# Sigmoid attention and a gated feed-forward in one kernel: four changes of order and buffer around a TensorE that is already full

## The chip, the cores and the metric

The kernel runs on one core of one Trainium2 chip. The metric is the device time of a run in microseconds (us). A run's span, from its first to its last instruction, is about 1.8 us shorter. Every run also lists its mean granted TensorE clock (1.0 is full speed).

## The reference

```python
# q, k, v: (8 batches, 12 heads, 448 positions, 64)
scores = scale * np.matmul(q, k.transpose(0, 1, 3, 2)) - np.log(448)
attn = 1.0 / (1.0 + np.exp(-scores))
attn_out = np.matmul(attn, v)
x = attn_out.transpose(0, 2, 1, 3).reshape(3584, 768)
gate = np.maximum(x @ w_gate, 0.0)          # 768 -> 1536
out = (gate * (x @ w_val)) @ w_out          # 1536 -> 768
```

## The kernel before

A block is four heads of one batch, so a batch has three blocks and a block has seven passes. A pass computes a tile of scores (four matmuls), and ScalarE turns it into sigmoids. Value matmuls follow some passes later and gather a block's seven passes in one value tile. The first batch's three blocks (21 passes) run alone. After that the feed-forward of batch b fills TensorE, and the attention of batch b + 1 is slipped in by visits of three passes. Six key and query blocks are transposed on TensorE (block 0's keys in two parts); the later ones are transposed by DMA.

PSUM has three two-bank buffers (`qkp`: scores, value tiles, some transposes) and two one-bank buffers (`wkp`: feed-forward tiles, early transposes, zero matmuls).

```python
    qkp = ctx.enter_context(tc.tile_pool(name="qkp", bufs=3, space=bass.MemoryType.PSUM))
    wkp = ctx.enter_context(tc.tile_pool(name="wkp", bufs=2, space=bass.MemoryType.PSUM))
    # ... cut ...
    def transposes(n: int, nm: str, *engines, cut=(0, NCH)):
        h16 = qk16.pop((nm, n))
        if n <= NBLK:
            tr = wkp.tile([P, NCH, 2, KC], FP16, tag="wk", name="tr")
        else:
            tr = qkp.tile([P, 2, 512], FP32, tag="qk", name="tr")[:, 0, 0 : S].bitcast(FP16)
        # ... seven transposes into tr, then VectorE copies tr to SBUF
    # ... cut: down(), the output matmuls of 128 rows; the very last 256 columns go in two parts
            nb = 2 if last and m0 else 1
            w = mn // nb
            ys = [wkp.tile([P, 512], FP32, tag="wk", name="y_ps") for _ in range(nb)]
    # ... cut: the start; fills are matmuls on zeros that keep TensorE busy
        new_fill()                       # a one-bank tile
        filler(*[512] * 10)
        # ... casts and transposes of block 0
        new_fill()                       # the other one-bank tile
        filler(128, 128, 128)
    # ... cut: the 21 passes of the first batch
        for i in range(NP0 + 2):
            # ... scores of pass i; values of pass i - 4, from pass 17 on of pass i - 2
            if i == 14:
                cast_qk(NBLK, "k", nc.vector)          # NBLK is 3: block 3
            if i == 15:
                transposes(NBLK, "k")
                cast_qk(NBLK, "q", nc.vector)
            if i == 16:
                transposes(NBLK, "q")
    # ... cut: what a visit sets off after its scores
        if c == 4 and NBLK < m < NPRO:                 # blocks 4 and 5
            transposes(m, "k")
            transposes(m, "q")
```

## Time and profile before

| | before |
|---|---|
| median of the three runs at hand | 436.0 us (433.4 to 436.61) |
| profiled run | 434.29 us, span 432.5, clock 1.000 |
| TensorE busy | 418.7 us of the span |
| stage in which TensorE has no gap | 66.26 to 426.66 |

A few words first. PSUM is the memory that TensorE writes to; an evacuation copies a finished tile out of it. A cast turns a loaded float32 tile into float16, and a transfer lands when its last bytes have arrived.

Three views carry the argument. A stage table gives the busy time of each engine between chosen instants. An engine's timeline gives start, length and instruction, and in brackets how long the engine had been idle and who released it. The chain of waits follows the last instruction back. Busy time hides the question here: TensorE is 97% busy, so only the few places where it (or, at the start, ScalarE) waits can be won. The prediction below shows those lines.

### The profile page before, as it was taken

Reading aid. Unit: us, or ns where it says so; the run is one execution under the profiler, and the core shown is the slowest. Engines: PE = TensorE matmul, PEld = TensorE weight load, DVE = VectorE, ACT = ScalarE, POOL = GpSimd, SP = SyncE. Lnnn points to the kernel's source line nnn. Section 1 sums busy time; section 2 is a strip of 40 time slices with the busy share of each in tenths; the row PEclk is TensorE's granted clock in tenths of the full one; section 3 lists DMA queues with packets and bytes.
Section 4 is the critical chain, followed back from the end, with each engine's and each line's share of the span. In section 5 each row is a group of like instructions: output and inputs, shape, how many; then the busy total and the mean of one; then the engine's idle time right before and its main releaser. Section 6 shows DMA issues by size and latency. Waiting matters only on the chain.

```text
span 432.5 us, 7873 instructions
## 1 busy us (share of the span) xinstructions
PE 418.7 (97%) x3282; PEld 216.6 (50%) x3282; DVE 165.9 (38%) x276; ACT 178.8 (41%) x217; POOL 102.6 (24%) x137
## 2 busy tenths in 40 slices
PE   7779899999999999999999999999999999999996
PEld 3334445545455445545455444554455544555553
DVE  3444442244322533243422444234432445235531
ACT  5962445553534353525253435352534352500000
POOL 2567783223110333004130142103330030000000
PEclk9999999999999999999999999999999999999999
DMA  8999996366625754286432766246444730030014
GB/s 302 384 386 385 392 356 182 104 175 167 170 74 107 179 155 144 75 202 176 109 101 73 208 171 170 50 106 185 137 149 111 162 88 0 19 94 0 2 36 109
DMA packets 64371, 66.96 MB, mean 155 GB/s; under 512 B 35792, under 2 KB 54608, under 8 KB 64336
## 3 DMA queue, kind: packets, MB, share of 16 engines
q1 hardware_dynamic: 63088, 64.63, 51.2%
q10 hardware_dynamic: 1248, 1.84, 1.2%
q8 instruction: 25, 0.41, 0.4%
q14 instruction: 10, 0.08, 0.1%
HBM read 47.19 MB, written 11.01 MB: 135 GB/s over the span
## 4 chain that ended last, share of the span: by engine, by line
PE 93%; DMA 3%; ACT 2%; DVE 1%; issue 1%; ACTq 0%
PE gv_ps L230 51%; PE y_ps L269 26%; PE qk_ps L171 8%; PE pv_ps L195 6%; DMA st_k<-in_k_dram 3%; ACT PT L181 2%; PE fill L357 1%; PE tr L157 1%; ACT xT L209 0%; DVE ysb L283 0%; DVE h16k L105 0%; DVE xT L211 0%; DVE gate_sb L247 0%; DVE h16q L105 0%; ACT kT L161 0%
## 5 line engine op out<-in xcount | busy, mean ns | idle before, releaser
L181 ACT ACTIVATE PT<-qk_ps,bias_t 128x896 f16<-128x896 f32 x168 | 159.4, 1008 | 194.5 <-PE qk_ps L171 194.5
L230 PE MATMUL gv_ps<-xT,wg 128*128 128x448 f16 x576 | 128.1, 353 | 0.6 <-DVE gate_sb L247 0.3
L230 PE MATMUL gv_ps<-xT,wv 128*128 128x448 f16 x576 | 126.8, 353 | 0.0
L269 PE MATMUL y_ps<-wo,hT 128*128 128x512 f16 (+2 forms) x684 | 113.8, 323 | 0.7 <-DVE ysb L283 0.7
L269 PEld LDWEIGHTS <-hT 128*128 128x128 f16 x684 | 64.5, 98 | 48.9 <-issue 7.2
L247 DVE TENSOR_SCALAR gate_sb<-gv_ps 128x448 f32<-128x448 f32 x96 | 59.9, 624 | 71.9 <-PE gv_ps L230 71.9
L254 DVE TENSOR_TENSOR hT<-gate_sb,gv_ps 128x448 f16<-128x448 f32 x96 | 59.6, 621 | 63.4 <-PE gv_ps L230 63.2
L230 PEld LDWEIGHTS <-wv 128*128 128x128 f16 x576 | 55.1, 98 | 55.1 <-issue 5.7
L230 PEld LDWEIGHTS <-wg 128*128 128x128 f16 x576 | 55.0, 98 | 55.0 <-issue 6.5
L283 DVE TENSOR_SCALAR ysb<-y_ps 128x512 f32<-128x512 f32 (+2 forms) x56 | 31.1, 556 | 105.7 <-PE y_ps L269 105.7
L105 POOL CAST h16q<-st_q 128x896 f16<-128x896 f32 x20 | 18.6, 930 | 223.2 <-DMA st_q<-in_q_dram 199.5
L171 PE MATMUL qk_ps<-qT,kT 64*64 64x448 f16 x672 | 48.5, 359 | 2.4 <-ACT PT L181 2.1
L195 PE MATMUL pv_ps<-PT,v 64*64 64x448 f16 x672 | 38.9, 350 | 0.9 <-ACT PT L181 0.8
L171 PEld LDWEIGHTS <-kT 64*64 64x64 f16 x672 | 16.2, 105 | 27.9 <-issue 21.7
L195 PEld LDWEIGHTS <-v 64*64 64x64 f16 x672 | 20.0, 107 | 12.9 <-issue 2.2
L209 ACT ACTIVATE xT<-pv_ps 128x448 f16<-128x448 f32 x43 | 21.0, 547 | 6.0 <-PE pv_ps L195 4.8
L281 ACT ACTIVATE ysb<-y_ps 128x128 f32<-128x128 f32 x1 | 0.3, 277 | 45.4 <-PE y_ps L269 45.4
L105 POOL CAST h16k<-st_k 128x896 f16<-128x896 f32 x20 | 18.6, 928 | 0.0
L112 POOL CAST v<-st_v 128x448 f16<-128x448 f32 x24 | 13.6, 565 | 13.0 <-DMA st_v<-in_v_dram 11.9
L113 POOL CAST v<-st_v 64x448 f16<-64x448 f32 x24 | 13.4, 557 | 1.5
L114 POOL CAST v<-st_v 64x448 f16<-64x448 f32 x24 | 13.3, 555 | 1.0
L137 POOL CAST wg<-st_wg 128x1536 f16<-128x1536 f32 x6 | 8.8, 1466 | 3.4 <-DMA st_wg<-in_moe_w_gate_dram 3.1
(26 smaller groups left out, 58.4 us busy)
## 6 DMA issues: line engine op xcount, KB each, us to landing
out_dram<-ysb SPq DMA_DIRECT2D x54, 192.0 KB, 2.7
st_q<-in_q_dram SPq DMA_DIRECT2D x23, 448.0 KB, 4.5
st_v<-in_v_dram SPq DMA_DIRECT2D x23, 448.0 KB, 5.3
st_k<-in_k_dram SPq DMA_DIRECT2D x22, 448.0 KB, 3.9
st_wg<-in_moe_w_gate_dram SPq DMA_DIRECT2D x6, 768.0 KB, 12.4
st_wu<-in_moe_w_val_dram SPq DMA_DIRECT2D x6, 768.0 KB, 12.2
st_wo<-in_moe_w_out_dram SPq DMA_DIRECT2D x6, 768.0 KB, 11.8
st_v<-in_v_dram ACTq DMA_DIRECT2D x1, 448.0 KB, 6.0
```

What stands on the lines that cost most here:

```text
L105: eng.tensor_copy(o, i)
L112: eng.tensor_copy(t[:, 0], st[:, 0])
L113: eng.tensor_copy(t[0:64, 1], st[64:128, 1])
L171: nc.tensor.matmul(ps[o : o + 64, bank, 0:S], kT[r : r + 64, c, h, :], qT[r : r + 64, :, h, :], start=True, stop=True, tile_position=(r, o ...
L181: nc.scalar.activation(pt[:], ps[:, :, 0:S], AF.Sigmoid, bias=bias_t[:], scale=qk_scale)
L195: nc.tensor.matmul(pv[o : o + 64, pr, 0:S], t[r : r + 64, pr, c * D : (c + 1) * D], pt[r : r + 64, pr, :], start=(c == 0), stop=(c == NCH ...
L209: nc.scalar.activation(x[:], pv[:, pr, 0:S], AF.Copy, scale=XSCALE)
L230: nc.tensor.matmul(begun[key][:, 0:S], w[j][:, dc, jj * P : (jj + 1) * P], xT[b, dc][:], start=(dc == 0), stop=(dc == NDC - 1),)
L247: nc.vector.tensor_scalar(out=g_sb[:], in0=gate[:, 0:S], scalar1=0.0, scalar2=None, op0=AOP.max)
L254: nc.vector.tensor_tensor(out=hT[f][:, o : o + S], in0=g_sb[:], in1=val[:, 0:S], op=AOP.mult)
L269: nc.tensor.matmul(y[:, 0:w], hT[f][:, o : o + P], wo[f // FG][:, f % FG, c0 : c0 + w], start=(f == 0), stop=(f == NFC - 1),)
L283: nc.vector.tensor_scalar(out=dst, in0=y[:, 0:w], scalar1=OUT_SCALE, scalar2=None, op0=AOP.mult)
```

## The change

The intent is to take waits away without taking work away: (1) the zero matmuls at the start write into the first value tile, not the one-bank buffers; (2) block 3's casts and transposes stand later in the queue, and its values are loaded behind the value weights; (3) the transposes of blocks 4 and 5 stand some 2 us behind a visit, not inside it; (4) the last output tile goes into a score tile.

```diff
@@ (1) the fills @@
-            nc.tensor.matmul(fill[-1][:, 0:w], zeros[:, 0:P], zeros[:, 0:w], start=True, stop=True)
+            nc.tensor.matmul(PT[0][:, 0, 0:w], zeros[:, 0:P], zeros[:, 0:w], start=True, stop=True)
@@ (2) block 3 @@
-        order = halves("g", 0) + [3] + halves("u", 0) + halves("g", 1) + halves("u", 1)
+        order = halves("g", 0) + ["kq"] + halves("u", 0) + ["v"] + halves("g", 1) + halves("u", 1)
-            if i == 14:
+            if i == 15:
                 cast_qk(NBLK, "k", nc.vector)
-            if i == 15:
-                transposes(NBLK, "k")
+            if i == 17:
                 cast_qk(NBLK, "q", nc.vector)
-            if i == 16:
-                transposes(NBLK, "q")
+                transposes(NBLK, "k")
@@ after the early gate matmuls of passes 18 and 21 @@
+            if i == 20:
+                transposes(NBLK, "q")
@@ first feed-forward tile: three value matmuls ahead of the gate, not four @@
-                yield from up(b, f, 4, 4)
+                yield from up(b, f, 4, 3)
@@ (3) visits @@
-            transposes(m, "k")
-            transposes(m, "q")
+            later.append(m)
...
-                    todo.pop(0)
+                    due = todo.pop(0) + 2.0
                     visit()
+                if later and t >= due:
+                    m = later.pop(0)
+                    transposes(m, "k")
+                    transposes(m, "q")
@@ (4) the end @@
-            ys = [wkp.tile([P, 512], FP32, tag="wk", name="y_ps") for _ in range(nb)]
+            if nb == 2:
+                yt = qkp.tile([P, 2, 512], FP32, tag="qk", name="y_ps")
+                ys = [yt[:, 0], yt[:, 1]]
+            else:
+                ys = [wkp.tile([P, 512], FP32, tag="wk", name="y_ps")]
@@ cut: helper code that follows from these @@
```

More of the change, by code (lines that the diff above doesn't have):

```diff
@@ L91, in load_block, with load_all @@
             staged[nm, n] = st
-    def load_all(n: int):
-        load_block(n, ("k", k, 0, NCH, nc.sync), ("q", q, 0, NCH, nc.sync), ("v", v, 0, NCH, nc.sync))
+    def load_all(n: int, names="kqv"):
+        for nm, src in (("k", k), ("q", q), ("v", v)):
+            if nm in names:
+                load_block(n, (nm, src, 0, NCH, nc.sync))
     def cast_qk(n: int, nm: str, *engines, cut=(0, NCH)):
@@ L187, in values @@
     def values(n: int, chunks):
-        if chunks[0] == 0:
+        if chunks[0] == 0 and n not in PT:
             PT[n] = qkp.tile([P, 2, 512], FP32, tag="qk", name="pv_ps")
@@ L328, in feed @@
             load_all(m + 1)
+    later: list = []
     valued: set = set()
@@ L351 @@
     nc.vector.memset(zeros[:], 0.0)
-    fill: list = []
     def filler(*widths):
+        if 0 not in PT:
+            PT[0] = qkp.tile([P, 2, 512], FP32, tag="qk", name="pv_ps")
         for w in widths:
-            nc.tensor.matmul(fill[-1][:, 0:w], zeros[:, 0:P], zeros[:, 0:w], start=True, stop=True)
-    def new_fill():
-        fill.append(wkp.tile([P, 512], FP32, tag="wk", name="fill"))
+            nc.tensor.matmul(PT[0][:, 0, 0:w], zeros[:, 0:P], zeros[:, 0:w], start=True, stop=True)
     with tc.manual_schedule():
@@ L380, in start_next @@
                 load_all(what)
-                if what > NBLK:
-                    cast_block(what)
-                else:
-                    cast_v(what, nc.gpsimd)
+                cast_block(what)
+            elif isinstance(what, str):
+                load_all(NBLK, what)
+                if what == "v":
+                    cast_v(NBLK, nc.gpsimd)
             else:
@@ L387, in start_next @@
                 cast_w(*what, nc.gpsimd)
-        new_fill()
         filler(*[512] * 10)
@@ L395 @@
         transposes(0, "k", nc.scalar, nc.vector, cut=(0, 2, 4))
-        new_fill()
         filler(128, 128, 128)
@@ L423 @@
                 transposes(n + 1, "k" if c == 3 else "q")
-            if i == 14:
+            if i == 15:
                 cast_qk(NBLK, "k", nc.vector)
-            if i == 15:
+            if i == 17:
+                cast_qk(NBLK, "q", nc.vector)
                 transposes(NBLK, "k")
-                cast_qk(NBLK, "q", nc.vector)
-            if i == 16:
-                transposes(NBLK, "q")
             if i in (18, 21):
                 gv_part(0, 0, wg, [0, 1] if i == 18 else [2, 3])
+            if i == 20:
+                transposes(NBLK, "q")
             if 11 <= i < NP0:
```

## The prediction

> **What bounds the kernel now.** I read the page's first rows, then the table of stages, then each engine's timeline in the stages where TensorE is not full. First the busy shares, the slices and the chain of waits:
>
> ```profile
> PE 418.7 (97%) x3282; PEld 216.6 (50%) x3282; DVE 165.9 (38%) x276; ACT 178.8 (41%) x217; POOL 102.6 (24%) x137
> ...
> PE   7779899999999999999999999999999999999996
> ...
> DMA  8999996366625754286432766246444730030014
> ...
> PE 93%; DMA 3%; ACT 2%; DVE 1%; issue 1%; ACTq 0%
> ```
>
> TensorE's row is full from the sixth slice to the last but one. The DMA row is full only in the first six slices (65 us). So the middle can be moved only by fewer or shorter matmuls, and the change has none. The table of stages (start:end, length, then busy us of PE, PEld, DVE, ACT and POOL with instruction counts, clock, DMA share, GB/s), whose borders I chose at events of the timeline, shows where there is room:
>
> ```profile
> 0.00:7.94 7.94, 6.56 (x34) 3.07 (x34) 2.08 (x6) 2.77 (x6) 1.29 (x8) 1.00 0.78 271
> 7.94:29.37 21.43, 15.63 (x212) 7.38 (x209) 10.04 (x18) 19.54 (x21) 12.20 (x15) 1.00 1.05 385
> 29.37:32.17 2.80, 2.21 (x14) 0.95 (x13) 1.25 (x2) 0.54 (x1) 1.80 (x2) 1.00 1.05 385
> 32.17:66.26 34.09, 32.27 (x248) 16.42 (x248) 16.19 (x26) 13.42 (x16) 26.46 (x25) 1.00 0.98 364
> 66.26:426.66 360.40, 360.40 (x2757) 187.41 (x2756) 135.32 (x223) 142.20 (x174) 60.83 (x90) 1.00 0.45 118
> 426.66:432.50 5.84, 1.67 (x25) 1.36 (x23) 0.98 (x2) 0.28 (x1) 0.00 (x0) 1.00 0.38 104
> ```
>
> From 66.26 to 426.66 TensorE has no gap at all: 360.4 us that the change cannot shorten. From 7.94 to 29.37 ScalarE's 21 sigmoids set the pace (19.54 of 21.43 us). From 32.17 to 66.26 TensorE lacks 1.8 us. The clock is 1.00 everywhere, so no idle gap costs clock.
>
> ScalarE's timeline in that second stage (start, us, engine, line; in brackets the idle before and its releaser):
>
> ```profile
> 7.94 3.70 ACT L181 ACTIVATE PT<-qk_ps,bias_t 128x896 f16<-128x896 f32 x4 [0.49 <-PE qk_ps L171]
> 11.99 10.93 ACT L181 ACTIVATE PT<-qk_ps,bias_t 128x896 f16<-128x896 f32 x12 [0.35 <-PE qk_ps L171]
> 23.11 1.01 ACT L181 ACTIVATE PT<-qk_ps,bias_t 128x896 f16<-128x896 f32 x1 [0.19 <-PE qk_ps L171]
> 24.92 1.01 ACT L181 ACTIVATE PT<-qk_ps,bias_t 128x896 f16<-128x896 f32 x1 [0.81 <-PE qk_ps L171]
> 26.47 2.90 ACT L181 ACTIVATE PT<-qk_ps,bias_t 128x896 f16<-128x896 f32 x3 [0.54 <-PE qk_ps L171]
> ```
>
> ScalarE starves five times. TensorE's timeline says why for the later gaps, for the visits of blocks 4 and 5, and for the end:
>
> ```profile
> 22.11 0.56 PE L157 MATMUL tr<-ident,h16k 128*128 128x128 f16 x7 [0.37 <-DVE h16k L105]
> ...
> 23.93 0.57 PE L157 MATMUL tr<-ident,h16q 128*128 128x128 f16 x7 [0.75 <-DVE h16q L105]
> ...
> 46.15 0.55 PE L157 MATMUL tr<-ident,h16k 128*128 128x128 f16 x7 [0.79 <-ACT PT L181]
> 47.05 0.55 PE L157 MATMUL tr<-ident,h16q 128*128 128x128 f16 x7 [0.35 <-ACT PT L181]
> ...
> 58.91 0.55 PE L157 MATMUL tr<-ident,h16k 128*128 128x128 f16 x7 [0.37 <-ACT PT L181]
> 59.78 0.55 PE L157 MATMUL tr<-ident,h16q 128*128 128x128 f16 x7 [0.32 <-ACT xT L209]
> ...
> 427.61 1.45 PE L269 MATMUL y_ps<-wo,hT 128*128 128x128 f16 x23 [0.73 <-DVE ysb L283]
> ```
>
> Block 3's transposes stand in TensorE's queue before their cast is there: the keys' transfer, queued at 9.66, lands only at 21.32. In the visits the transposes need a bank that a sigmoid is still reading. At the end the last tile needs the bank that VectorE is emptying.
>
> **What the Trainium skill says.** (1) "TensorE: Matmul & The Clock Gate", Wait — 56ns, not 53.3ns?: back-to-back matmuls start N / 2.4 GHz + about 2.5 ns apart when warm. The trace agrees: the last feed-forward's 144 gate and value matmuls (N 448) take 27.24 us in the chain, 189 ns each (page: 189), and seven 128-wide transposes in a row 0.39 us (47.05 to 47.44), 56 ns each. (2) Same page, Step-by-step: only weight loads are pulled ahead; matmuls keep program order. So a waiting transpose holds up the score behind it, as the 0.75 us wait at 23.93 and ScalarE's 0.81 us gap show. (3) "ScalarE: Activation LUTs", What ACT_TABLE_LOAD costs: an activation with a pointer bias takes 280 ns + 0.833 ns an element, 1026 ns for 896, and successive ones overlap by 93 ns. The trace has 1008 ns, and twelve in 10.93 us: (10.93 - 1.01) / 11 = 0.90 us pitch, which I use. (4) "Trainium Kernel Development and Optimization", Key Constraints: all issuing queues share the same 16 DMA engines. Here the loads move 385 GB/s with the DMA share at 1.05, so until about 63 us landing times follow from bytes queued ahead.
>
> **The change part by part.** I built the changed kernel and read its order and its list of waits.
>
> *Zero matmuls in the first value tile.* The fills leave the two one-bank buffers, so block 1's key transposes no longer wait (1.5 us, at 11.07) for the copy of block 0's late keys. The fifth score then waits only for that copy, which ends at 11.02: score 11.08, sigmoid about 11.5 in place of 11.99. ScalarE's 0.35 us gap closes, and the sigmoids run at the pitch. The price is that two score buffers are left in place of three from the start; a score takes 0.38 us against a 0.90 us pitch, so they suffice.
>
> *Block 3's order.* In the queue keys and queries already stood ahead of the value weights; what moves is block 3's values, to behind two 0.79 MB halves. That brings those halves forward by 0.46 MB / 385 GB/s = 1.2 us (from 25.83 and 27.79). The casts and transposes move later: key transposes to pass 17, query transposes to pass 20. Pitch from 7.94: pass 17's sigmoid starts at 7.94 + 17 x 0.90 = 23.3 and ends at 24.3. By the list of waits score 18 takes the buffer of pass 17, since the new value tile takes that of pass 16. So it starts at 24.35, and its sigmoid at 24.8, 0.55 late. Two more pitches and one duration: 24.8 + 1.8 + 1.0 = 27.6, where it is 29.37 now. Gain 1.75 us. The path from there to 32.17 (value matmuls, VectorE and ScalarE scaling, last gate matmul, gate activation: 2.8 us) stays. The fourth value matmul moves behind the last gate matmul, into the 0.63 us that VectorE's gate step takes, so it is free.
>
> *Transposes between visits.* Now, from the end of a visit's scores (44.59 + 0.69 = 45.28) to the next gate matmul (47.44) are 2.16 us, of which 14 x 0.056 = 0.78 is work: 1.38 lost. Second visit: 58.19 + 0.19 = 58.38 to 60.17, 1.79 - 0.78 = 1.01 lost. In the changed order some 11 matmuls (2.1 us) stand between, by when two sigmoids have ended and freed their banks. VectorE's two copies (1.25 us) go ahead of a product and may push the next value group by 0.2. Gain 2.2 us.
>
> *End in a score tile.* The list of waits shows the last tile's first matmul free of VectorE. It starts a pitch (0.22) after the matmul before it, near 426.7 in place of 427.61. Gain 0.9 us.
>
> *Taken back.* The last output weights land by DMA and are cast at 62.99 to 64.46. The first output matmuls, at 66.26 now, move up by 1.75 + 2.2 to 62.3, and the 11th, which needs that half, to 62.3 + 10 x 0.217 = 64.5. So some 0.15 us is lost.
>
> Sum: 1.75 + 2.2 + 0.9 - 0.15 = 4.7 us, 1.1% of 436.
>
> **Rivals.** *The DMA takes the place of the waits removed.* For it: the DMA is full to 65 us and the last weights clear the need by nothing. Were the landings 1 us later, 1 us would go; the gain falls to 3.5. Against: the bytes and their order after block 3 are the same. *Two score buffers starve ScalarE from the start,* or the waits at passes 17 to 20 are longer than 0.55 us: the stage gains 0.5 to 1, in all 3.5 to 4, time 432.3. For it: value matmuls, a transpose and a buffer meet at pass 17. Against: twelve sigmoids already run without a gap with a value tile open. *ScalarE gives all its lost time back:* 7.94 + 20 x 0.90 + 1.0 = 26.95, 2.4 us; with everything else 5.4 us, time 430.6. *The waits were hidden anyway:* against it, the chain of waits runs through each of them and nothing behind is slack. For a loss over 2% (8.7 us) a new stall would have to repeat in every batch, and the later batches have the same instructions and waits.
>
> **Range and chances.** Off the median of 436.0: 436.0 - 4.7 = 431.3. The three runs of before spread 3.2 us (433.4 to 436.6), as large as most of my terms. The rivals give 430.6 to 432.5; with about 1.5 us for the spread the range is 429.0 to 433.3. Faster by over 2% needs 427.3 or less, nearly twice the gain: 0.05. Slower: 0.01.
>
> **What would show it.** Right: ScalarE's first 21 sigmoids in two or three runs, the last ending near 27.6; no gap before block 3's transposes; gate matmuls in full flow from about 30.4; the transposes of blocks 4 and 5 without a wait on a sigmoid; the first output matmuls near 62.3; no wait on VectorE before the last tile; span near 427.8. Wrong: an output matmul waiting over 1 us for a weight cast, sigmoid gaps over 1 us near passes 17 to 20, or the full stretch longer than 360.4 us.

## The result

| | before | changed |
|---|---|---|
| median of the runs of this comparison | 435.29 us (433.4 to 436.61, 4 runs) | 430.12 us (430.01 to 430.52, 4 runs) |
| profiled run | 434.29 us, span 432.5, clock 1.000 | 430.22 us, span 428.4, clock 0.998 |

The ratio is 0.9886, with a 95% interval of 0.9845 to 0.9927. A ratio here is the mean time of one kernel's fast runs over that of the other's of the same rounds, so it isn't quite the ratio of the medians quoted.

First the page of the changed kernel: busy time, and the chain that ended last by engine.

```profile
PE 418.1 (98%) x3282; PEld 216.5 (51%) x3282; DVE 166.5 (39%) x276; ACT 178.5 (42%) x217; POOL 102.2 (24%) x137
...
PE 93%; ACT 3%; DMA 2%; DVE 1%; issue 0%; ACTq 0%; DVEq 0%
```

The work is the same, 418 us; only the waits around it went. The stage table of the changed kernel, with borders at the same events as in the prediction's table (first sigmoid, end of the 21st, second gate tile, first output matmul, 360.40 us on, end):

```profile
0.00:7.79 7.79, 6.31 (x34) 3.10 (x34) 2.07 (x6) 2.74 (x5) 1.29 (x8) 1.00 0.78 272
7.79:27.85 20.06, 15.69 (x212) 7.42 (x209) 10.97 (x18) 19.32 (x21) 10.77 (x13) 1.00 1.05 385
27.85:30.65 2.80, 2.36 (x13) 0.96 (x13) 1.25 (x2) 0.55 (x2) 2.57 (x4) 1.00 1.05 384
30.65:62.53 31.88, 31.88 (x249) 16.19 (x249) 15.82 (x26) 13.61 (x16) 24.47 (x23) 1.00 1.05 389
62.53:422.93 360.40, 360.40 (x2758) 187.54 (x2757) 135.36 (x223) 142.01 (x174) 63.12 (x91) 1.00 0.45 119
422.93:428.40 5.47, 1.50 (x25) 1.32 (x23) 0.98 (x2) 0.28 (x1) 0.00 (x0) 0.82 0.41 111
```

Stage by stage against before the lengths change by -0.15, -1.37, 0, -2.21, 0 and -0.37 us, together -4.1, which is 432.5 - 428.4. In the fourth stage TensorE's busy time now equals the stage's length. The 0.82 of the last stage costs nothing: the clock is at 0.50 from about 426.4 on, and the last matmul ends at 424.43. ScalarE's first 21 sigmoids in the changed kernel's timeline:

```profile
7.79 16.52 ACT L183 ACTIVATE PT<-qk_ps,bias_t 128x896 f16<-128x896 f32 x18 [0.49 <-PE qk_ps L173]
24.96 2.89 ACT L183 ACTIVATE PT<-qk_ps,bias_t 128x896 f16<-128x896 f32 x3 [0.65 <-PE qk_ps L173]
```

Of the gaps one is left, before pass 18. TensorE's transposes of blocks 4 and 5, which waited 0.79, 0.35, 0.37 and 0.32 us:

```profile
45.49 0.55 PE L159 MATMUL tr<-ident,h16k 128*128 128x128 f16 x7
45.88 0.55 PE L159 MATMUL tr<-ident,h16q 128*128 128x128 f16 x7
...
57.54 0.55 PE L159 MATMUL tr<-ident,h16k 128*128 128x128 f16 x7
57.93 0.55 PE L159 MATMUL tr<-ident,h16q 128*128 128x128 f16 x7
```

They have no bracket any more. Last, the end, from the timeline of all engines: the last two evacuations before, then the changed kernel (ACTq is ScalarE's own queue issuing a transfer):

```profile
429.04 0.28 ACT L281 ACTIVATE ysb<-y_ps 128x128 f32<-128x128 f32 x1 [45.42 <-PE y_ps L269]
429.09 0.29 DVE L283 TENSOR_SCALAR ysb<-y_ps 128x128 f32<-128x128 f32 x1 [1.53 <-PE y_ps L269]
...
423.85 0.55 ACTq L295 DMA_DIRECT2D out_dram<-ysb  x1
424.73 0.28 ACT L287 ACTIVATE ysb<-y_ps 128x128 f32<-128x128 f32 x1 [44.85 <-PE y_ps L275]
425.04 0.29 DVE L289 TENSOR_SCALAR ysb<-y_ps 128x128 f32<-128x128 f32 x1 [1.22 <-ACT ysb L287]
```

This is new. The two last evacuations ran side by side before; now VectorE's is released by ScalarE's.

### The profile page after: what moved, and what is told of

The parts are those of the page before. It is cut to its first block, busy times and chain, and to the rows that moved or that the text cites. A ratio compares the mean times of both kernels' runs of the same rounds, so it can differ in the third digit from the quotient of the medians.

```text
span 428.4 us, 7873 instructions
## 1 busy us (share of the span) xinstructions
PE 418.1 (98%) x3282; PEld 216.5 (51%) x3282; DVE 166.5 (39%) x276; ACT 178.5 (42%) x217; POOL 102.2 (24%) x137
## 4 chain that ended last, share of the span: by engine, by line
PE 93%; ACT 3%; DMA 2%; DVE 1%; issue 0%; ACTq 0%; DVEq 0%
PE gv_ps L232 51%; PE y_ps L275 26%; PE qk_ps L173 8%; PE pv_ps L197 7%; ACT PT L183 3%; DMA st_q<-in_q_dram 2%; PE tr L159 1%; DVE ysb L289 0%; DVE gate_sb L249 0%; DVE xT L213 0%; DVE h16q L107 0%; ACT L367 0%; ACT xT L211 0%; ACTq L295 0%; ACTq L90 0%
## 5 line engine op out<-in xcount | busy, mean ns | idle before, releaser
L139 POOL CAST wv<-st_wu 128x1536 f16<-128x1536 f32 x6 | 8.8, 1467 | 5.7 <-DMA st_wu<-in_moe_w_val_dram 5.7
```

## The experiments

Twelve runs on three chips, each of six timed runs unless said. "Full clock" means a mean granted clock of 0.997 or more; the rest are called halved, as their profiles show stretches at 0.50. Spans are in us.

| run | chip | full-clock spans: median (range), runs | halved | ratio to before |
|---|---|---|---|---|
| before, same rounds | A | 431.7 (431.7 to 431.9), 3 of 11 | 8 | |
| fills undone, first | A | 428.4 (428.3 to 428.5), 5 | 1 | 0.991 |
| block 3 undone | A | 429.2 (429.1 to 430.1), 4 | 2 | 0.9939 |
| visits undone | A | 430.3 (429.9 to 430.5), 6 | 0 | 0.9955 |
| end undone | A | 428.6 (428.1 to 429.1), 5 | 1 | 0.9908 |
| before, same rounds | B | 431.8 (431.6 to 432.0), 4 of 11 | 7 | |
| fills alone | B | 431.7 (431.5 to 432.0), 5 | 1 | 0.9975 |
| block 3 alone | B | 431.1 (430.9 to 431.1), 3 | 3 | 0.9959 |
| end in two tiles | B | 427.9 (427.4 to 428.0), 5 | 1 | 0.9881 |
| and without ScalarE's issue | B | 427.8 (427.7 to 429.1), 6 | 0 | 0.9885 |
| before, same rounds | C | 431.8 (431.7 to 432.0), 6 of 11 | 5 | |
| before again | C | 431.7 (431.7 to 431.9), 3 | 3 | 1.0 |
| changed again | C | 427.9 (427.7 to 428.1), 4 of 4 | 0 | 0.9903 |
| fills undone, second | C | 428.45 (428.4, 428.5), 2 | 4 | 0.9926 |
| three mends | C | see below | | 1.0013 |

All outputs are right.

### The fills put back

```diff
-            nc.tensor.matmul(PT[0][:, 0, 0:w], ...)
+            nc.tensor.matmul(fill[-1][:, 0:w], ...)   # and the two new_fill() calls
```

> The changed kernel with the zero matmuls back in the two one-bank buffers. My theory: the fifth score again waits behind block 1's key transposes, which wait about 1.5 us for a VectorE copy; ScalarE's gap of 0.35 us before its fifth sigmoid comes back and, as the passes for block 3 stay late, it is not absorbed: span 0.3 to 0.45 us longer than the changed kernel's 428.4. Rival: the later gap before pass 18 absorbs it, and the span stays at 428.4 within 0.1.

The profiled run had a span of 429.3, but its clock stood at 0.50 for 3.4 us, so it can't be set against 428.4. The five full-clock runs gave 428.4, no longer than the changed kernel's 428.2 to 428.7 in the first comparison, whose chip isn't on record. Taken alone this run decided nothing.

### Block 3 put back

```diff
+            if i == 14: cast_qk(NBLK, "k", ...)
+            if i == 15: transposes(NBLK, "k"); cast_qk(NBLK, "q", ...)
+            if i == 16: transposes(NBLK, "q")
# the lines of passes 15, 17 and 20 removed, the load order and up(b, f, 4, 4) as before
```

> The changed kernel with block 3 as before: load order, passes 14, 15 and 16 for its casts and transposes, four early value matmuls. My theory: the transposes wait again for the landing of block 3's keys near 21; that landing anchors the rest, so the gain of the zero matmuls is lost with it: the first 21 sigmoids end near 29.2 and the span is 1.4 us longer than 428.4. Rival: the parts are independent, and only 1.0 us comes back. On the spread: the kernel before ran between 433.4 and 436.6, the changed one between 430.0 and 430.5. If the exposed landing makes the spread, this kernel's timed runs spread over 2 us or more; if it has another cause, it spreads as little as the changed one, under 1 us.

TensorE's timeline of this run has block 3's waits back:

```profile
21.59 0.56 PE L157 MATMUL tr<-ident,h16k 128*128 128x128 f16 x7 [0.58 <-DVE h16k L105]
...
23.41 0.93 PE L157 MATMUL tr<-ident,h16q 128*128 128x128 f16 x7 [0.75 <-DVE h16q L105]
```

The second group takes 0.93 us, not 0.57: the clock halved at 23.4 and stayed so until 26.8. The sigmoids ended at 29.80 (29.2 expected at full clock). At full clock the span is 429.2, which is 1.3 above the changed kernel on chip C. On chip A itself the run with only the end undone, less its 0.37, gives 428.2 for the changed kernel, and so 1.0. So these runs don't tell the theory's 1.4 from the rival's 1.0. The timed runs spread over 1.7 us, less than the 2 I had set.

### Transposes back inside the visits

```diff
+            transposes(m, "k")
+            transposes(m, "q")
-            later.append(m)
```

> The changed kernel with the transposes of blocks 4 and 5 directly in their visits. My theory: the four waits for a sigmoid or a scaling come back, span 2.2 us longer (430.6), all of it before the first output matmul (near 64.7 in place of 62.5). Rival: with the visits earlier by 1.5 us the DMA's landings bound this stage, and less than 1 us comes back.

The first output matmul came at 64.67, and the first wait is the old one, to the digit:

```profile
44.37 0.55 PE L159 MATMUL tr<-ident,h16k 128*128 128x128 f16 x7 [0.79 <-ACT PT L183]
```

From the first gate activation to the first output matmul there are 34.77 us here and before, and 32.55 in the changed kernel: 2.22 us. No wait for a transfer took its place. This stage doesn't depend on the start or on the clock there, so its size is settled.

### The end put back in the one-bank buffers

```diff
+            ys = [wkp.tile([P, 512], FP32, tag="wk", name="y_ps") for _ in range(nb)]
```

> The changed kernel with the last tile's two parts in the one-bank buffers again. I had predicted 0.9 us for this part; the trace of the changed kernel shows the matmuls moved up by 0.88 but the stage shorter by only 0.37, as ScalarE's last evacuation starts 0.3 late and VectorE's waits for it. My theory: span 0.37 us longer than 428.4. Rival (the trace of one run misleads, and the part is worth what I predicted): 0.9 us longer.

From VectorE's last 512-wide evacuation to the end of the span: 5.65 us here, 5.63 before, 5.28 in the changed kernel. The part is worth 0.37 us, as expected from the trace, not 0.9. This run's profile also shows the halved clock best, in a stage table with borders a window apart (clock is the third number from the right):

```profile
3.95:7.37 3.42, 2.63 (x29) 1.44 (x28) 1.90 (x5) 2.12 (x4) 0.46 (x1) 1.00 1.06 378
7.37:10.78 3.41, 1.95 (x24) 1.06 (x23) 1.59 (x4) 2.85 (x4) 1.21 (x3) 1.00 1.06 385
10.78:14.19 3.41, 3.41 (x35) 1.54 (x39) 1.28 (x3) 2.19 (x3) 1.93 (x4) 0.50 1.06 383
```

"TensorE: Matmul & The Clock Gate" (What's actually happening) in the Trainium skill describes a free-running window of 3.4 us after which an idle array drops to half clock. The length agrees with the trace: 3.41 us at 0.50. The window ahead was 57% busy (1.95 of 3.41), so "idle" is less than it sounds.

### The fills alone, on the kernel before

> The kernel before with the zero matmuls moved to the first value tile and nothing else. My theory: the gap before the fifth sigmoid closes, but block 3's transposes still wait for the landing of block 3's keys (near 21.3), so the gain turns into a longer wait there: span within 0.15 us of 432.5. Rival: the parts are independent: span 0.4 us shorter.

The edit is part (1) of the diff alone. At full clock 431.7 against 431.8: the gain is absorbed, as the theory said. Where it is absorbed isn't shown, since the profile is of a halved run (span 433.6, 6.8 us at 0.50).

### Block 3 alone, on the kernel before

> The kernel before with block 3's part alone: load order, later casts and transposes, three early value matmuls. My theory: 21 sigmoids lose only the 0.35 us gap near the fifth and one gap near pass 18: span about 1.0 us shorter than 432.5. Spread of the timed runs: under 1 us if the exposed landing of block 3's keys makes the spread of the kernel before; 2 us or more if not.

The edit is part (2) alone. At full clock 431.1 against 431.8, so 0.7 us, not 1.0. Three of six runs were halved, and the runs spread over 1.2 us (432.7 to 433.87), between the two bounds that I had set, so the spread decides nothing. But the halvings stayed without the exposed landing, so it is not their only cause. The profile has this kernel's fill waits instead, with the clock halved at 11.

### The end in two score tiles

```diff
-                yt = qkp.tile([P, 2, 512], FP32, tag="qk", name="y_ps")
-                ys = [yt[:, 0], yt[:, 1]]
+                ys = [qkp.tile([P, 2, 512], FP32, tag="qk", name="y_ps")[:, 0] for _ in range(nb)]
```

> The changed kernel with the last tile's two parts in two score tiles in place of the two banks of one. My theory: VectorE's last evacuation no longer waits for ScalarE's, starts near the end of the last matmul (424.4) and ends near 424.75; but ScalarE's still starts late, at about 424.73, behind its own DMA issue, and the transfer it starts is then the last: span 0.2 to 0.3 us shorter than 428.4. Rival: the wait for ScalarE is a bookkeeping artefact and nothing changes.

```profile
424.37 0.29 DVE L288 TENSOR_SCALAR ysb<-y_ps 128x128 f32<-128x128 f32 x1 [0.65 <-PE y_ps L274]
424.64 0.28 ACT L286 ACTIVATE ysb<-y_ps 128x128 f32<-128x128 f32 x1 [44.85 <-PE y_ps L274]
```

VectorE's evacuation is released by TensorE again, 1.34 us after its 512-wide one began (423.03); it was 1.92 in the changed kernel and 2.22 before. So the matmuls had gained 0.88, which is the predicted 0.9. ScalarE still starts 0.27 late. From the 512-wide evacuation the end takes 4.97 us in place of 5.28: 0.31 us won.

### And the first 512 columns issued by SyncE

```diff
-                for half, eng in enumerate((nc.sync, nc.scalar if last else nc.sync)):
+                for half, eng in enumerate((nc.sync, nc.scalar if last and m0 else nc.sync)):
```

> As the run before, and the output of the first 512 columns of the last tile issued wholly by SyncE, so that ScalarE has no DMA issue ahead of its evacuation. My theory: both evacuations start at 424.45 and span is 0.5 to 0.6 us shorter than 428.4, which is what I had predicted for this part. Rival: SyncE's issues of 0.5 us each now delay the last transfer instead, and the gain is 0.2 us or less.

```profile
423.96 0.28 ACT L286 ACTIVATE ysb<-y_ps 128x128 f32<-128x128 f32 x1 [44.53 <-PE y_ps L274]
424.01 0.29 DVE L288 TENSOR_SCALAR ysb<-y_ps 128x128 f32<-128x128 f32 x1 [0.65 <-PE y_ps L274]
```

ScalarE now starts 1.28 us after the 512-wide evacuation (422.68), where it took 1.61 with a DMA issue ahead of it: its own issue was what held it. But the stage is 5.12 us, longer than with two tiles alone. SyncE's three issues for this tile now run until 425.14, and the last transfer to start is theirs. The rival was right.

### Both kernels again

> The kernel before once more, for a second profile. The profile that I predicted from has block 1's keys and queries ready at 9.59 and 10.13, block 3's keys at 21.32 and the last sigmoid ending at 29.37, span 432.5; the timed runs at full clock since then span 431.6 to 432.0. My theory: that profile caught late landings. This one, if at full clock, has block 1 ready at 8.7 to 9.2, the sigmoids end near 28.6 and the span is 431.6 to 432.0. Rival: sigmoids end near 29.4 again and something later is shorter. In about half of the runs of before TensorE's clock is halved for some microseconds near 11 or 23 (mean clock 0.996 or less); then the span is longer.

> The changed kernel once more, on the same chip as the kernel before, for the true size of the gain. My theory: spans of 428.1 to 428.7 at full clock, 3.5 us shorter than those of before at full clock (2.2 between the visits, 0.9 in block 3's stage, 0.4 at the end), and 4 to 5 us in the mean, since at most one run of six has the halved clock. Rival: as many runs with the halved clock as before (about half), and the mean gain is 3.5 us too.

The kernel before was at full clock, span 431.7. ScalarE's timeline from its fifth sigmoid on:

```profile
11.64 11.84 ACT L181 ACTIVATE PT<-qk_ps,bias_t 128x896 f16<-128x896 f32 x13 [0.39 <-PE qk_ps L171]
24.15 1.01 ACT L181 ACTIVATE PT<-qk_ps,bias_t 128x896 f16<-128x896 f32 x1 [0.67 <-PE qk_ps L171]
25.70 2.90 ACT L181 ACTIVATE PT<-qk_ps,bias_t 128x896 f16<-128x896 f32 x3 [0.54 <-PE qk_ps L171]
```

They end at 28.60, not 29.37. The casts of block 1 began at 9.03 and 9.78 and block 3's at 20.58 (9.59, 10.13 and 21.32 in the first profile). So the first profile had caught late landings. The changed kernel on the same chip:

```profile
6.59 3.70 ACT L183 ACTIVATE PT<-qk_ps,bias_t 128x896 f16<-128x896 f32 x4 [0.49 <-PE qk_ps L173]
11.03 12.73 ACT L183 ACTIVATE PT<-qk_ps,bias_t 128x896 f16<-128x896 f32 x14 [0.74 <-PE qk_ps L173]
24.41 2.89 ACT L183 ACTIVATE PT<-qk_ps,bias_t 128x896 f16<-128x896 f32 x3 [0.65 <-PE qk_ps L173]
```

The first sigmoid comes 0.96 us sooner, mainly as the first ten zero matmuls took 3.78 us, not 4.45 (3.67 to 4.45 in the profiles, whatever the kernel). Much of that is lost by the fifth sigmoid, which waits for block 1's queries: it starts 1.86 us after VectorE begins their cast in both profiles of before, and 1.39 in this one (9.64 to 11.03). That 0.47 us is what the fills' part is worth in time at this sigmoid. At full clock the two kernels are 431.8 and 427.9, 3.9 us apart; the ratio 0.9903 means 4.2 us in the mean of all runs.

### The fills put back, again

> The changed kernel with the zero matmuls back, once more, for a profile at full clock and more runs to count. Two of my readings are at odds: the gap of 0.35 us before the fifth sigmoid should come back, but the timed runs at full clock differ from the changed kernel by 0.1 us. My theory now: with block 1 ready by 9.2 and 9.7, VectorE's copy ends near 10.6 and the fifth sigmoid starts near 11.5, 0.15 us or less behind the pitch; only late landings, as in the profile of before, make it 0.35 to 0.45. On the clock: without the move TensorE idles near 10, and two of six runs or more have the halved clock. Rival: none or one of six, as with the move.

```profile
10.67 0.64 PE L159 MATMUL tr<-ident,h16k 128*128 128x128 f16 x7 [2.18 <-DVE kT L165]
```

Against the changed kernel on the same chip the two full-clock runs are 0.55 us longer (428.45 against 427.9), near the 0.47 from the timelines. So the times speak against my revised theory of 0.15 or less; the first one (0.3 to 0.45) was nearer. The profile, of a halved run, can't show it. Four of six runs were halved, three of them for some 0.9 us more (429.3 and 429.4); the fourth (428.5) was no longer. In the profiled one the clock drops at 11.0, just after TensorE had waited 2.18 us for a buffer.

### Three mends at once

```diff
-            while done <= i - (4 if i < NP0 - 4 else 2):
+            while done <= i - (4 if i < NP0 - 3 else 2):
# the last tile in two score tiles, and one 256 KB transfer by SyncE for its first 512 columns
```

> The changed kernel with three mends: value matmuls of block 2 start one pass later (18), the last tile's parts in two score tiles, the output of its first 512 columns as one transfer of SyncE. My theory: the score of pass 18 takes the buffer of pass 16 and ScalarE's gap of 0.65 us goes, so the 21 sigmoids run in one piece (19.1 us in place of 19.9 to 20.1); both last evacuations start with the end of the last matmul and the end is 0.5 us shorter. Span 427.0 to 427.4, 0.9 to 1.2 below the changed kernel's at full clock. Rival: the value tile's later start delays the last values, and only the end's 0.5 us is won.

It lost: 434.43 us, ratio 1.0013. Two mends failed.

```profile
25.99 1.91 ACT L183 ACTIVATE PT<-qk_ps,bias_t 128x896 f16<-128x896 f32 x2 [0.82 <-PE qk_ps L173]
```

The gap moved from pass 18 to pass 19 and grew to 0.82 us. That score now stands behind three passes of values and two gate matmuls in TensorE's queue. At the end both evacuations did start on time (424.45 and 424.51), but the last transfers took 5.4 and 7.2 us to land in place of 2.2 and 1.9. The last stage is 9.73 us. The merged transfer is the only edit left that could do it. From 429.0 to 431.0 the DMA share is 0.13 at 48 GB/s: by that share, about two of the 16 DMA engines were at work, where the loads had 385 GB/s at 1.05. So the transfer seems to have run on few engines; why it did was not tested. The mean clock of these runs is lowered by that long tail, so they aren't counted as full or halved. The best version remains the changed kernel with two tiles at its end, ahead by 0.31 us in its last stage alone; its timed runs don't tell it from the changed kernel.

### How often the clock was halved

| fills in the value tile | block 3 late | runs halved | kernels |
|---|---|---|---|
| no | no | 23 of 39 | before, and again |
| no | yes | 8 of 18 | fills undone twice, block 3 alone |
| yes | no | 3 of 12 | block 3 undone, fills alone |
| yes | yes | 2 of 32 | changed (0 of 8), visits undone, end undone, two tiles, SyncE's issue |

All 16 full-clock runs of before have spans of 431.6 to 432.0; its halved ones reach 436.9. So most of the spread of before goes with the halved clock, and both early parts of the change make it rarer (with runs at 0.996 counted as full, the first row is 14 of 39 and the last 1 of 32). That they do it by shortening TensorE's waits near 10 and 22 fits the profiles, but was only argued.

The halved clock isn't the whole spread. Five of the 23 halved runs of before have spans of 431.8 to 432.0 too; single full-clock runs of other kernels stray upwards (430.1 with block 3 undone, 429.1 with the end undone); and two device times lie over 3 us above their span (433.82 and 436.02).

The order of instructions isn't the whole cause either. The five profiles halved near 11 are of runs whose first ten zero matmuls took 3.67, 3.79, 3.84, 3.91 and 3.91 us, and their clock dropped at 10.76, 11.00, 11.10, 11.25 and 11.26: the moment of the drop follows the length of the start. Of the eight profiles with 4.37 to 4.45 us none dropped there (block 3 undone dropped at 23.42), nor did the one other with a short start (3.78, changed again). And at full clock the first profile of before holds a stretch just as thin, 1.92 of 3.41 us busy from 7.70 on. So where the windows fall, which differs from run to run, seems to decide together with the waits; no run here sets it.

## Why the prediction was right, and where it was not

The time, 430.12, lies inside 429.0 to 433.3, 1.2 below the 431.3 predicted. That owes something to luck. In the pair of profiles the change gave 4.1 us, not 4.7. Taken off the profiled run's own 434.29, the 4.7 would have made 429.6, and 430.22 was measured. I took it off a median of 436.0, and the medians then differed by 5.2 (435.29 to 430.12), as more than the counted waits went.

- **Zero matmuls and block 3:** 1.75 predicted, 1.52 in the pair of profiles (start and sigmoids together). The fifth sigmoid came nearly where predicted (11.58 for 11.5), and the buffer read from the list of waits did leave a gap at pass 18: 0.65 us idle. The prediction's 0.55 is a slip: its own times make it 24.8 - 24.3 = 0.5 idle, or 0.66 behind the pitch (24.8 - 24.14). The first 18 sigmoids came at 0.91 us each ((16.52 - 1.01) / 17), not 0.90, and all ended at 27.85, not 27.6. In runs at full clock on one chip it is less, 1.3 (28.60 to 27.30), because the profile that I took as typical had late landings.
- **Visits:** 2.2 predicted with VectorE's copies taken off, 2.22 measured. The two stretches on TensorE's timeline, each less its 0.78 of work, gave 2.39; whether VectorE's copies took the missing 0.17 was not traced.
- **The end:** "Gain 0.9 us" failed in size. The matmuls moved up by 0.88. I let the end move with them, and did not ask what the evacuations would meet: ScalarE's own DMA issue, now just ahead of its evacuation, and a tile shared by two readers. 0.37 was left.
- **Taken back:** 0.15 predicted, nothing measured. The last weight cast ended at 64.19, and the 11th output matmul needed it at 62.53 + 2.17 = 64.70.
- **The rivals:** the DMA did not become the bound, two score buffers sufficed but for pass 18, and the waits were not hidden.
- **Not foreseen:** I wrote that no idle gap costs clock, from one profile at 1.00, which was too little to say so. In 23 of 39 runs of before the clock was halved for some time. This makes the mean gain larger than the waits alone: 4.2 against 3.9 us on chip C. In the first comparison it was about 5.0; the clocks of its early runs aren't listed, so the share there stays open.

## What to carry to other kernels

When the main engine is full, look for instructions that stand in its queue before their data or buffer is there, and move them back by as long as the release takes: that gave 2.22 us as computed. When matmuls at the end come sooner, follow them to the last transfer: an evacuation can meet a DMA issue on its own queue, or wait for another engine's read of the same tile. And take more than one profile of a stage that hangs on landings or on the clock.

## What the Trainium skill lacked or had wrong

- "TensorE: Matmul & The Clock Gate": it names an idle window of about 3.4 us before the clock is halved, and does not say how busy a window may be. Windows 57% busy (1.95 of 3.41 us) and 55% busy (1.88 of 3.40, block 3 undone) were followed by 3.4 us at 0.50, while a stretch 56% busy (1.92 of 3.41 us, before) was not.
- The same page puts the penalty of the ramp at the start under 1% of a typical span and advises not to fit to a count of slow matmuls. It gives no count of how often one kernel's clock is halved later on, or of how the order of early instructions changes that: 23 of 39 runs of the kernel before had one, with spans up to 436.9 against 431.6 to 432.0 at full clock, and 2 of 32 with both early parts changed.
- "Trainium Kernel Development and Optimization", Key Constraints: issuing from several engines saves issue time. It lacks the price: an issue of 0.55 us on ScalarE's queue held the evacuation behind it, which began 1.61 us after its reference and 1.28 without.
